# Decode attention on one Trainium2 core: TensorE's code made smaller and brought in by an early jump, with the first load held until TensorE has begun

## The chip, the cores and the metric

The kernel runs on one core of one Trainium2 chip. The metric is the device time of one execution in microseconds; a lower time is better. A kernel was run several times, always beside runs of the kernel before on the same chip. A profile is one execution, so its numbers belong to one run and not to the median run. The span of a profile is about 1.4 us shorter than the measured time of the same execution (before: span 1291.5 us, median time 1292.9 us).

Names: TensorE (PE) multiplies, and PEld is its weight load; VectorE is DVE, ScalarE is ACT, GpSimd is POOL and SyncE is SP. The profile's page counts 16 DMA engines. A *transfer* here is one load issued by SyncE, and a *packet* is one entry of the trace's DMA list, taken as one piece of a transfer on one DMA engine. For keys and values a packet is 64 KiB, and each transfer has 128 of them and ends with 16 completion packets of 4 bytes, taken here as one for each engine. The trace does not name the engine of a packet. So "the latest engine" below is the last of the 16 completion packets of a transfer, and that each engine takes a fixed share of every transfer (128 / 16 = 8 packets) is a reading: it fits these counts and a lateness that stays the same over hundreds of microseconds (in the kernel before the latest engine is 1.57 us late at 238.0 us and 1.56 at 1263.6).

## The reference

```python
def reference(A_x, A_k_cache, A_v_cache, A_wq, A_wo, B_x, B_w1, B_b1, B_w2, B_b2):
    def _A_ref(x, k_cache, v_cache, wq, wo):           # x: 8 x 1 x 576, caches: 8 x 32 x 4096 x 128
        q = (x @ wq).reshape(B, Sq, H, Dh).transpose(0, 2, 1, 3)
        scores = jnp.einsum("bhqd,bhkd->bhqk", q, k_cache) * (Dh ** -0.5)
        p = _softmax(scores, axis=-1)
        o = jnp.einsum("bhqk,bhkd->bhqd", p, v_cache)
        return o.transpose(0, 2, 1, 3).reshape(B, Sq, H * Dh) @ wo
    def _B_ref(x, w1, b1, w2, b2):                     # w1: 576 x 4608, w2: 4608 x 576
        y = _layernorm(x, axis=-1)
        return _gelu(y @ w1 + b1) @ w2 + b2
    x = A_x
    xn = _layernorm(x, axis=-1)
    return x + _A_ref(xn, A_k_cache, A_v_cache, A_wq, A_wo) + _B_ref(xn, B_w1, B_b1, B_w2, B_b2)
```

All tensors are bf16. The caches are 537 MB of the 557 MB that are read, so this is a kernel of reading memory once.

## The kernel before

SyncE issues every large load, in this order, on one queue: the query weights, the weights of the first layer, then keys and values of tiles 0 to 31, then the second layer's weights and the output weights in four parts. All of them land in one buffer (`ring`) that holds about three of the large transfers (keys or values of one tile), so a load is issued only when an older one has been used up.

```python
    od.load("sync", "wq", ring[:, 0:WQ_END], wq_v)       # transfer 0, moved ahead of the start barrier
    first = od.name
    od.load("sync", "w1", ring[:, W1_AT:RING], w1_v)     # transfer 1
    ahead(nc, ENG.SP, [first, od.name], "InstDrain")
    load_kv(k_v, 0, 0)                                   # transfer 2: keys 0
    # ...
    for token in (wq_read, *head_done):                  # the query weights have been read
        od.wait("sync", token)
    load_kv(v_v, 0, 1)                                   # transfer 3: values 0
    for token in mlp_done:                               # the whole head is done
        od.wait("sync", token)
    for t in range(1, NT):
        sy.wait_ge(sem["kf"], NX * (t - 1) + 2)          # TensorE has eaten 2 of 8 blocks of keys t-1
        load_kv(k_v, t, 0)                               # transfer 4 is keys 1
        sy.wait_ge(sem["vf"], t)                         # TensorE is through with values t-1
        load_kv(v_v, t, 1)                               # transfer 5 is values 1
```

The *head* is the work before the first tile: layer norms, the queries, their broadcast to 128 partitions, and the first layer of the MLP. TensorE's code for it is written out:

```python
    def queries(e):                                      # 36 matmuls; in the trace 4 narrow ones in 0.43 us
        for c in range(WC):
            wv = wq_sb[:, c, :].rearrange("p (x m d) -> p m x d", m=M, d=Dh)
            for m in range(M):
                i = e.matmul(S_ps[0][m * MP:(m + 1) * MP, :], lhsT=xT[:, c, :], rhs=wv[:, m], ...)
    # ...
    for b in range(B):                                   # broadcasts: 8 x 4 matmuls, before the first layer
        # ...
        pe(["q", "sel"], [key], broadcast)
        act([key], [f"qb{b}"], lambda e: e.activation(out=dst, in_=t, func=ACT.Copy))
    head_done = [od.last(e) for e in ("tensor", "vector", "scalar")]
    for c in range(WC):                                  # first layer: 9 x 6 matmuls
        pe(["yT", "w1"], ["h_ps"], lambda e, c=c: layer(e, yT[:, c, :], w1_sb[:, c, :], ...))
```

Then VectorE multiplies each key tile by the queries in 8 blocks (the *products*), TensorE sums them, ScalarE takes the exponentials and TensorE multiplies by the values. TensorE goes over the 32 tiles in a loop. Its last 72 + 8 + 64 matmuls are the second layer and the output projection.

The softmax here doesn't subtract the row's maximum and nothing guards it: scores larger than these inputs give would overflow.

## Time and profile before

| | before |
|---|---|
| time, median of 6 runs | 1292.91 us (1292.82 to 1293.04) |
| span of the profile | 1291.5 us |
| read from memory | 556.94 MB, 431 GB/s over the span |
| busy: TensorE, VectorE, ScalarE | 57%, 64%, 4% |

The first lines are of the profile's page: its span, the busy share of the DMA engines in 40 slices, and the DMA queues with packets, MB and share of the time of 16 engines.

```profile
span 1291.5 us, 14658 instructions
...
DMA  9999999999999999999999999999999999999998
...
q1 hardware_dynamic: 10368, 556.93, 99.7%
q8 instruction: 3, 0.05, 0.0%
...
q14 instruction: 1, 0.01, 0.0%
```

The load queue (q1) keeps the 16 engines busy for 99.7% of the span. A 64 KiB packet takes 2.418 us in the trace, so 16 engines move 16 x 65,536 B / 2.418 us = 434 GB/s, and nothing but the two ends and the unevenness of the engines is left to win. The lines "instruction" are the packets whose kind in the trace is "instruction", taken here as code that is brought to an engine. The trace has their times in the span: three of 16 KiB at 29.93, 75.96 and 1287.07 us, each taking 1.0 to 1.1 us, and one of 8 KiB at 52.15 us, taking 0.31 us.

The next view cuts the end into stretches of 0.5 us. The columns are the length, then the busy time of PE, PEld, DVE, ACT and POOL with the number of instructions, TensorE's granted clock, the mean busy share of the DMA engines, and GB/s.

```profile
1287.20:1287.70 0.50, 0.18 (x4) 0.00 (x0) 0.00 (x0) 0.00 (x0) 0.00 (x0) 1.00 0.18 74
1287.70:1288.20 0.50, 0.00 (x0) 0.00 (x0) 0.00 (x0) 0.00 (x0) 0.00 (x0) 1.00 0.19 74
1288.20:1288.70 0.50, 0.39 (x8) 0.30 (x10) 0.00 (x0) 0.00 (x0) 0.00 (x0) 1.00 0.07 28
```

A share of 0.18 or 0.19 is 3 engines of 16. So for the last microsecond of loading 13 engines are done and three are not. The packets show since when. The table holds how late each engine completes a transfer, against the median of the 16; only the four latest are shown.

```
kernel before, completion of a transfer by its latest four engines, us over the median of 16
transfer 1 (first-layer weights)   25.1 us:  0.15  0.20  0.21  0.46
transfer 2 (keys 0)                44.5 us:  0.15  0.16  0.41  1.41
transfer 3 (values 0)              63.8 us:  0.12  0.13  1.31  1.41
transfer 4 (keys 1)                83.2 us:  0.10  1.31  1.42  1.53
transfer 12                       238.0 us:  0.14  1.35  1.45  1.57
```

After each of the first three instruction packets (29.9, 52.2, 76.0 us) one more engine is 1.3 to 1.5 us late. It stays late to the end (0.13, 1.34, 1.45, 1.56 us at 1263.6 us). This fits the fixed share read above and a queue that never pauses (busy for 99.7% of the span), so that it cannot catch up.

The chain of work that ended last shows what this costs (start, duration, what):

```profile
1259.74 28.52 DMA ring<-in_A_wo_dram
1288.26 0.04 issue
1288.31 1.29 PE acc L374 x18
```

TensorE waits until 1288.26 us for a part of the output weights, and 18 matmuls, a cast and the store follow. What the latest engine loses there is lost for the kernel: in the profile after the change this landing is 1.43 us later and the span 1.4 us longer.

Last, the times at which SyncE issues its loads, and the head's main steps. These lines are of the timeline (start, duration, engine, line, operation).

```profile
0.00 0.38 SPq L96 DMA_DIRECT2D ring<-in_A_wq_dram  x1
...
53.53 0.33 SPq L271 DMA_DIRECT2D ring<-in_A_k_cache_dram  x1
74.24 0.33 SPq L271 DMA_DIRECT2D ring<-in_A_v_cache_dram  x1
```

```profile
13.84 4.01 PE L367 MATMUL s_ps<-ring 128*32 128x512 bf16 x36 [1.36 <-DVE quad L354]
...
18.55 0.41 PE L394 MATMUL oT_ps<-ring 128*64 128x256 bf16 x4 [0.36 <-ACT ring L385]
...
26.02 0.85 PE L414 MATMUL o_ps<-ring 128*32 128x384 bf16 x3 [2.80 <-DMA ring<-in_B_w_dram]
...
46.82 6.70 DVE L559 TENSOR_TENSOR ring<-ring,qb 128x4096 bf16<-128x4096 bf16 x3 [0.32 <-DVE hT_sb L445]
```

The queries take 4 us, the broadcasts start at 18.55 us while the first layer's weights are still on their way (they land at about 25.6 us), and VectorE's first product starts at 46.82 us. Keys 1 are issued at 53.53 us. The first engine is through with the transfer before it (values 0) at 63.48 us, so the queue has a *margin* of 63.48 - 53.53 = 9.95 us. Values 1 have 82.81 - 74.24 = 8.57 us. In the steady state the margins are 10.2 and 8.8 us.

### The profile page before, as it was taken

The numbers are of one execution on the slowest core, as the hardware profiler recorded it, in microseconds if no ns is written. First come the engines' busy times: TensorE is split into PE (matmuls) and PEld (weight loads), VectorE is DVE, ScalarE is ACT, GpSimd is POOL, SyncE is SP. The second block draws the span as 40 slices with busy tenths as digits, with TensorE's granted clock in tenths as the row PEclk, the third lists the DMA queues.
The fourth block names the chain that finished last, engine by engine and source line by source line (L and its number), as shares of the span: only waits on it lengthen the run. The fifth ranks groups of instructions, "written<-read, shape, count | busy, mean of one in ns | idle before, by whom it ended". The sixth has DMA issues, their size and how long they took to land. (4 is left out here: it accounts for less than half of the span.)

```text
span 1291.5 us, 14658 instructions
## 1 busy us (share of the span) xinstructions
PE 736.8 (57%) x4707; PEld 322.3 (25%) x4707; DVE 829.4 (64%) x740; ACT 56.8 (4%) x181; POOL 2.4 (0%) x12
## 2 busy tenths in 40 slices
PE   4654565554565554665554565554566554565557
PEld 1222232222222222222222232222222222222223
DVE  2655677655677655677655677655677655577654
ACT  2000000000000000000000000000000000000000
POOL 0000000000000000000000000000000000000000
PEclk8778887778887777887777887778887777888779
DMA  9999999999999999999999999999999999999998
GB/s 419 441 427 440 430 428 449 422 428 449 422 428 449 422 430 447 422 436 440 424 436 438 426 438 434 428 442 428 428 449 422 428 449 422 428 449 422 430 447 350
DMA packets 10410, 557.02 MB, mean 431 GB/s; under 512 B 1163, under 2 KB 1188, under 8 KB 1446
## 3 DMA queue, kind: packets, MB, share of 16 engines
q1 hardware_dynamic: 10368, 556.93, 99.7%
q8 instruction: 3, 0.05, 0.0%
q10 hardware_dynamic: 38, 0.02, 0.0%
q14 instruction: 1, 0.01, 0.0%
HBM read 556.94 MB, written 0.01 MB: 431 GB/s over the span
## 5 line engine op out<-in xcount | busy, mean ns | idle before, releaser
L643 PE MATMUL s_ps<-ring,ident 128*128 x2048 | 544.5, 423 | 514.1 <-PEq L641 513.1
L559 DVE TENSOR_TENSOR ring<-ring,qb 128x4096 bf16<-128x4096 bf16 x256 | 579.2, 2283 | 281.6 <-DMA ring<-in_A_k_cache_dram 281.3
L643 PEld LDWEIGHTS s_ps<-ring,ident 128*128 128x128 bf16 x2048 | 217.4, 106 | 828.3 <-issue 678.5
L534 DVE TENSOR_REDUCE sc<-s_ps 128x32 f32<-128x512 f32 x256 | 171.8, 684 | 0.0
L662 PE MATMUL o_ps<-ring,ebd 128*32 128x512 bf16 x2048 | 116.4, 380 | 0.0
L546 DVE TENSOR_TENSOR ebd<-es,head 128x1536 bf16<-128x1536 bf16 x64 | 77.9, 1218 | 0.0
L569 DVE RECIPROCAL rec<-tot_ps 128x8 f32<-128x8 f32 x32 | 6.6, 208 | 110.7 <-PE oT_ps L670 110.7
L582 ACT ACTIVATE es<-sc 128x192 bf16<-128x192 f32 x64 | 19.8, 310 | 1104.2 <-DVE sc L534 1104.2
L662 PEld LDWEIGHTS o_ps<-ring,ebd 128*32 128x32 bf16 x2048 | 51.6, 97 | 62.5 <-issue 13.6
L670 PE MATMUL oT_ps<-selc,ob 128*128 128x8 f32 x256 | 33.9, 259 | 12.3 <-ACT ob L586 12.3
L670 PEld LDWEIGHTS oT_ps<-selc,ob 128*128 128x128 f32 x256 | 31.0, 191 | 15.2 <-ACT ob L586 15.2
L586 ACT ACTIVATE ob<-o_ps 128x512 f32<-128x512 f32 x32 | 19.1, 597 | 80.2 <-PE o_ps L662 80.2
L425 DVE TENSOR_SCALAR ring<-ring 96x384 f32<-96x384 f32 x2 | 0.7, 352 | 26.4 <-ACT ring L424 26.4
L545 DVE TENSOR_TENSOR Es<-Ep 128x1 f32<-128x1 f32 x32 | 5.1, 160 | 13.3 <-ACT es L582 13.3
L666 PEld LDWEIGHTS tot_ps<-headf,Es 128*128 128x128 f32 x64 | 9.5, 187 | 13.6 <-issue 13.6
L666 PE MATMUL tot_ps<-headf,Es 128*128 128x8 f32 x64 | 12.4, 266 | 0.0
L582 ACT ACTIVATION_READ_ACCUMULATOR es<-sc 128x1 f32 x64 | 11.9, 186 | 0.0
L414 PE MATMUL o_ps<-ring 128*32 128x384 bf16 x27 | 7.8, 860 | 2.8 <-DMA ring<-in_B_w_dram 2.8
L574 DVE TENSOR_TENSOR Ox<-on,quad 128x32 bf16 x32 | 6.2, 192 | 4.8
L414 PE MATMUL s_ps<-ring 128*32 128x384 bf16 x27 | 7.9, 862 | 0.0
L374 PE MATMUL acc<-ring,hT_sb 128*8 128x288 bf16 x72 | 6.0, 335 | 2.8 <-DMA ring<-in_B_w_dram 2.8
L336 PE MATMUL tot_ps<-ident,ring 40*128 40x16 bf16 x9 | 0.7, 204 | 11.8 <-DVE ring L314 11.8
(76 smaller groups left out, 61.2 us busy)
## 6 DMA issues: line engine op xcount, KB each, us to landing
ring<-in_B_w_dram SPq DMA_DIRECT2D x2, 5184.0 KB, 25.2
ring<-in_A_wq_dram SPq DMA_DIRECT2D x1, 4608.0 KB, 13.7
ring<-in_A_wo_dram SPq DMA_DIRECT2D x1, 1728.0 KB, 28.6
ring<-in_A_wo_dram SPq DMA_DIRECT2D x1, 1584.0 KB, 26.5
ring<-in_A_wo_dram SPq DMA_DIRECT2D x1, 1008.0 KB, 28.5
ring<-in_A_k_cache_dram SPq DMA_DIRECT2D x32, 31.9
ring<-in_A_v_cache_dram SPq DMA_DIRECT2D x32, 30.5
ring<-in_A_wo_dram SPq DMA_DIRECT2D x1, 288.0 KB, 28.8
```

Source lines behind the costliest of these rows:

```text
L414: i = e.matmul(h_ps[j][s * MP:(s + 1) * MP], lhsT=lhsT, rhs=wv[:, r0:r0 + HK, :], **flags)
L534: ins = ve.tensor_reduce(out=sc[:, n * CB:(n + 1) * CB], in_=bank_of(x).rearrange("p (c d) -> p c d", d=DL), axis=AX.X, op=ALU.add)
L546: ve.tensor_tensor(out=ebd[:, ja:jb], in0=es[:, a:b].rearrange("p (j c) -> p j c", c=4).unsqueeze(2) .to_broadcast([P, nj, G, 4]), in1=hea ...
L559: ve.tensor_tensor(out=k, in0=k, in1=qb[:, bass.ds(t, 1), :].to_broadcast([P, CB, Dh]), op=ALU.mult,).then_inc(sem["prod"], 1)
L569: ve.reciprocal(out=rec[:], in_=tot_ps[:, :G]).then_inc(sem["rec"], 1)
L574: ve.tensor_tensor(out=Ox[:, bass.ds(t, 1)].rearrange("p o g m -> p (o g) m"), in0=on[:].unsqueeze(2).to_broadcast([P, G, M]), in1=quad[:] ...
L582: sa.activation(out=es[:, a * CB:b * CB], in_=sc[:, a * CB:b * CB], func=ACT.Exp, scale=scale, accum_out=Ep[:, i:i + 1]).then_inc(sem["x"], 1)
L586: sa.activation(out=ob[:].rearrange("r c d -> r (c d)"), in_=o_ps, func=ACT.Copy).then_inc(sem["ob"], 1)
L643: ins = te.matmul(to, lhsT=idn, rhs=k[:, :, d * DL:(d + 1) * DL], start=(d == 0), stop=(d == Dh // DL - 1))
L662: ins = te.matmul(o_ps[m * MP:(m + 1) * MP, :], lhsT=ebd[:, j].rearrange("p g c -> p (g c)"), rhs=vals[:, c:c + 4, :], start=(j < M), stop ...
L666: te.matmul(tot_ps[:, :G], lhsT=Es[:].to_broadcast([P, P]), rhs=headf[:], start=True, stop=True).then_inc(sem["vf"], 1)
L670: ins = te.matmul(oT_ps[:, :G], lhsT=ob[:, c, :], rhs=selc[:, c, :], start=(c == 0), stop=(c == 3))
```

## The change

The intent is to bring TensorE's code in before the first load takes the DMA engines, so that no instruction packet falls among the loads (four do in the kernel before, at 29.93, 52.15, 75.96 and 1287.07 us). The change makes TensorE's code smaller with two register loops, jumps at the start to the last block and back, gives hints where the code of TensorE and VectorE ends, and lets SyncE's first load wait for TensorE's first instruction. The broadcasts move behind the first layer. The diff is cut to its core:

```diff
-    HS, HJ = 3, 2                                     # ... first layer in 6 groups of 384 columns
+    HK = NB // P                                      # ... now 5 groups, of 512 and one of 256 columns
+    te.sem_inc(sem["go"])                             # TensorE's first instruction
+    tensor_last = nc.mark_branch_hint_location(ENG.PE)
+    vector_last = nc.mark_branch_hint_location(ENG.DVE)
+    go = nc.sync.wait_ge(sem["go"], 1).ins.name
     od.load("sync", "wq", ring[:, 0:WQ_END], wq_v)
-    ahead(nc, ENG.SP, [first, od.name], "InstDrain")
+    ahead(nc, ENG.SP, [go, first, od.name], "InstDrain")
@@ queries: a loop; full-width matmuls on zero-padded weights
-        for c in range(WC):
-            for m in range(M):
-                i = e.matmul(S_ps[0][m * MP:(m + 1) * MP, :], lhsT=xT[:, c, :], rhs=wv[:, m], ...)
+                e.matmul(S_ps[0], lhsT=xTz[:, bass.ds(at + (M - 1 - m) * MP, P)], rhs=wv[:, m], ...)
+        (at, w), close = looped("queries", WC - 1, at=(M * MP, M * MP), w=(HQ, HQ))
+        part(at, w, False)
+        close()
@@ broadcasts: a loop of 8 turns, after the first layer
+    def broadcasts(e):
+        (at,), close = looped("broadcast", B, at=(0, MQ))
+        e.wait_ge(sem["free"], 1).then_inc(sem["free"], -1)
+        for v in range(2):
+            for k in reversed(range(NG)):
+                i = e.matmul(t[:(k + 1) * MQ, v * NH2:(v + 1) * NH2, :],
+                    lhsT=selz[:, bass.ds(at + (v * B + 1 - k) * MQ, (k + 1) * MQ)], rhs=q_v[:, k], ...)
+        i.then_inc(sem["full"], 1)
+        close()
@@ the end of the code
-    te.br("head")
+    te.br("tour")                                     # jump to the last block first
+    ve.br("vector_end").branch_hint(vector_last)
+    te.br("tensor_end").branch_hint(tensor_last)
+    block("tour")
+    later(main.bb, nc.cur_bb.bb, ENG.PE)              # TensorE's part of the start barrier stands here
+    te.br("head")
+    block("tensor_end")
```

## The prediction

> **What bounds the kernel now.** The DMA. The page gives 431 GB/s over the 1291.5 us span, 9 in all but one DMA slice, and the load queue 99.7% of 16 engines' time. A 64 KiB packet takes 2.42 us, so 16 engines move 433 GB/s and the 556.9 MB need 1286 us. TensorE is busy 57%, VectorE 64%, which waits 281 us for keys (waits view). Only the ends and the lateness of single DMA engines are left to win.
>
> **What the change aims at.** The DMA-queue part of the page lists instruction packets: three of 16 KiB on queue 8, at 29.9, 76.0 and 1287.1 us by the trace's packets, and one of 8 KiB on queue 14 at 52.2. [...] After each of the first three, one more DMA engine is late: landings lie within 0.5 us at 25 us, then one is 1.4 us behind at 44, two at 64, three (1.35, 1.45, 1.57 us) at 83, and so to the end[...]. In the windows view 3 of 16 engines (share 0.18) still work from 1287.2 to 1288.2. The last chain is: output weights land at 1288.26, 1.29 us of matmuls, a 0.45 us cast, the store. The fetches cost about 1.4 us of it.
>
> The change shrinks TensorE's code (about 790 instructions to 679[...]), jumps to its last block first, hints the ends of TensorE's and VectorE's code, and holds the first load until TensorE starts, so that fetches use idle DMA engines.
>
> **Costs.**
> - Hold: the first load issues at 0.00, TensorE's first instruction stands at 0.32. Estimate +0.35 us, not hidden.
> - The barrier waits for TensorE's jump[...]; keys 0 is queued at 1.26 and needed at 25: hidden.
> - Head: query matmuls lose their four-way concurrency (four in 0.43 us), 4 us become about 13, ending near 27; the first layer starts at 27 to 29 instead of 26 and takes 13 us as before. The broadcasts (5.3 us, before hidden behind the w1 load) come after it, in a register loop of some 1.3 us a turn, tied to ScalarE's 0.6 us copies. VectorE's first product moves from 46.8 to about 54 us. Slack: keys 1 are issued at 53.5 with the queue busy to 63.8, values 1 at 74.2 with it busy to 83.2; less 1 us from issue to packet, 7 to 8 us is hidden, just what I expect. Estimate +0.3 us of bubble on average, up to 3.
>
> **Sum.** 1292.9 - 1.4 + 0.35 + 0.3 = 1292.15; I lean a little lower, as the hold may cost less: predicted 1291.9 us, 80% range 1290.7 to 1293.6. Faster by over 2%: 0.01; within 2%: 0.98; slower by over 2%: 0.01.
>
> **What shows it right.** No instruction packets between the first load and the end; all 16 engines of the last transfers landing within about 0.5 us; no 3-engine tail in the windows view; the first product near 54 us; values 1 issued before 82.
>
> **What would make it wrong.** VectorE's or another fetch stays: the slowest engine is still 1.4 us late and nothing is won (about 1293.3). The early fetch collides with the first packets. The head slips over 8 us: DMA idles near 64 or 83 us, and the time rises by the excess.

The -1.4 rests on the lateness of the engines in the trace of the kernel before (1.35 to 1.57 us). The estimates start from that trace: +0.35 from TensorE's first instruction at 0.32 us; 13 us for the queries from 36 matmuls in 4.01 us, four in 0.43 us; 1.3 us a turn from ScalarE's copies of 0.60 us; 1 us from issue to packet from the first load (issued at 0.00, first packet at 1.008 us). How 13, 1.3 and +0.3 follow is not said.

## The result, and the profile after

| | before | after |
|---|---|---|
| time, median of 6 runs | 1292.91 us | 1294.17 us |
| lowest to highest | 1292.82 to 1293.04 | 1293.28 to 1297.37 |
| span of the profile | 1291.5 us | 1292.9 us |
| 16 KiB and 8 KiB instruction packets in the span | 3 and 1 | 1 and 0 |

The ratio of the times is 1.0012, with a 95% interval of 0.9999 to 1.0025. Ratios here are the mean time of one kernel's fast runs over that of the other's of the same rounds, so they are not quite the ratio of the medians. The median lies 1.3 us higher and above the predicted range, and the runs scatter over 4 us instead of 0.2. The intervals of all ratios here are 0.0013 to 0.0016 wide to each side (1.7 to 2 us), wider than most differences of this document. That the change is slower rests on the single runs (the fastest after, 1293.28 us, is above the slowest before, 1293.04) and on the traces.

These are the page's lines on the span and the queues after the change:

```profile
span 1292.9 us, 14775 instructions
...
q1 hardware_dynamic: 10368, 556.93, 99.7%
q8 instruction: 1, 0.02, 0.0%
```

One packet is left of four. VectorE's of 8 KiB is gone (it is VectorE's by x_cut against x_cut_hint: there at 49.6 us, not there with VectorE's hint) and so are two of the 16 KiB, TensorE's (none is left in x_small, with TensorE's code cut further). The one left is the early fetch; in the trace it runs from 1.537 to 2.963 us. This is after the first load's packets have started (the first at 1.297 us, nine by 1.537), so the two overlap. The order of events at the start, from the trace's instructions and packets:

```
kernel after, the start
0.203  TensorE adds to "go"
0.283  SyncE issues the first load (0.00 in the kernel before)
0.471  TensorE's jump to its last block; it takes 3.626 us
1.297  the first packets of the first load start
1.537  instruction packet, 16 KiB, takes 1.426 us
4.32   the start barrier releases all engines (1.18 in the kernel before)
```

```
kernel after, completion of a transfer by its latest four engines, us over the median of 16
transfer 0 (query weights)   13.2 us:  0.11  0.20  0.24  0.99
transfer 3 (values 0)        64.1 us:  0.11  0.19  0.23  1.04
```

There is now one late engine and not three, but the latest is still 1.04 us behind, and all 16 have been held back by 0.28 us. At 64 us the latest engine of the kernel after stands at 65.16 us and that of before at 65.26 us. Two of the fetches that are saved lie before this point. They are worth 0.1 us, with the hold and the early fetch taken off.

The second part of the answer is in the issue times of SyncE (timeline), and in the head:

```profile
0.28 0.38 SPq L96 DMA_DIRECT2D ring<-in_A_wq_dram  x1
...
61.35 0.33 SPq L294 DMA_DIRECT2D ring<-in_A_k_cache_dram  x1
82.57 0.33 SPq L294 DMA_DIRECT2D ring<-in_A_v_cache_dram  x1
```

```profile
14.78 10.34 PE L413 MATMUL s_ps<-ring 128*128 128x512 bf16 x36 [2.28 <-DMA ring<-in_A_wq_dram]
...
27.05 1.08 PE L446 MATMUL o_ps<-ring 128*32 128x512 bf16 x4 [1.59 <-DMA ring<-in_B_w_dram]
...
40.90 5.51 PE L468 MATMUL b_ps<-ring 128*128 128x256 bf16 x16
...
47.36 5.50 PE L468 MATMUL b_ps<-ring 128*128 128x256 bf16 x16 [0.95 <-PEq L465]
...
55.10 2.29 DVE L627 TENSOR_TENSOR ring<-ring,qb 128x4096 bf16<-128x4096 bf16 x1 [0.31 <-DVE hT_sb L513]
```

The queries take 10.3 us instead of 4.0. The first layer starts 1 us later and ends about as long after. The broadcasts, which were hidden behind the load of the first layer's weights, now take two stretches of 5.5 us at 40.9 and 47.4 us, with nothing to hide behind. The first product starts at 55.10 us, 8.3 us later than before. Keys 1 are issued 7.8 us later and values 1 8.3 us later. Their margins shrink from 9.95 to 63.68 - 61.35 = 2.33 us and from 8.57 to 83.43 - 82.57 = 0.86 us. VectorE shows the same from the other side: what it waits for between its first product and 112 us, first before, then after (engine, line, what it waits for, us in all, times, longest).

```profile
DVE ring L559 <- DMA ring<-in_A_k_cache_dram: 8.9, 1, 8.9
```

```profile
DVE ring L627 <- DMA ring<-in_A_k_cache_dram: 0.4, 1, 0.4
```

With a margin of 0.86 us the queue runs dry. The first packets of values 1, in the trace, start only 1.21 us after the issue, and they are longer than usual:

```
kernel after, packets of values 1 (64 KiB each): start, duration in us
83.778  3.006
83.849  3.278
83.957  3.233
84.149  2.556
...
84.740  2.713
85.149  2.975          the last of the 16 first packets; all 16 take 2.740 on average
86.702  2.418          the second packets are as usual
```

The engines thus lose time twice: they stand still (0.37 us on average and at most 0.7, if they restart in the order in which they finished), and the 16 first packets take 0.3 us longer on average and up to 0.86 us. The second loss does not need the first. At keys 1, with a margin of 2.33 us, the three engines that finish values 0 first go on without a pause, and still their packets take 2.80, 2.88 and 2.96 us; the longest of that transfer takes 3.46 us, and the mean completion is 0.46 us later there already. The mean completion of values 1 moves by 0.70 us in this one transfer. The latest engine goes from 0.05 us ahead of before (keys 1) to 0.98 us behind. Between 200 and 262 us, in a stretch with no lack of work (margins 9.3 to 10.9 us), another 0.45 us is lost on the latest engine: 91 packets there take over 2.45 us, up to 2.66, while the kernel before has none in that stretch. After that nothing more is lost: the difference of the latest engine is +1.42 us from 470 us to the end.

The windows of the end and the chain of work that ended last answer to the lines shown of before:

```profile
1288.20:1288.70 0.50, 0.50 (x12) 0.24 (x6) 0.00 (x0) 0.00 (x0) 0.00 (x0) 1.00 0.82 325
1288.70:1289.20 0.50, 0.13 (x4) 0.00 (x0) 0.00 (x0) 0.00 (x0) 0.00 (x0) 1.00 0.34 131
1289.20:1289.70 0.50, 0.00 (x0) 0.00 (x0) 0.00 (x0) 0.00 (x0) 0.00 (x0) 1.00 0.11 42
```

```profile
1261.24 28.46 DMA ring<-in_A_wo_dram
1289.69 0.04 issue
1289.74 1.29 PE acc L425 x18
```

The tail of single late engines is still there (0.34, then 0.11), and the same part of the output weights lands at 1289.69 us instead of 1288.26: +1.43 us. The 18 matmuls are the same. So the whole loss of the profiled run (1.4 us of span) was made before 280 us and then carried to the end.

### The profile page after: what moved, and what is told of

The parts are those of the page before. It is cut to its first block, busy times and chain, and to the rows that moved or that the text cites. A ratio compares the mean times of both kernels' runs of the same rounds, so it can differ in the third digit from the quotient of the medians.

```text
span 1292.9 us, 14775 instructions
## 1 busy us (share of the span) xinstructions
PE 741.7 (57%) x4698; PEld 324.8 (25%) x4698; DVE 829.6 (64%) x740; ACT 56.6 (4%) x181; POOL 3.4 (0%) x13
## 3 DMA queue, kind: packets, MB, share of 16 engines
q1 hardware_dynamic: 10368, 556.93, 99.7%
## 5 line engine op out<-in xcount | busy, mean ns | idle before, releaser
L713 PE MATMUL s_ps<-ring,ident 128*128 x2048 | 535.8, 417 | 515.9 <-PEq L711 515.8
L713 PEld LDWEIGHTS s_ps<-ring,ident 128*128 128x128 bf16 x2048 | 214.8, 105 | 824.0 <-issue 670.8
L637 DVE RECIPROCAL rec<-b_ps 128x8 f32<-128x8 f32 x32 | 6.7, 208 | 110.7 <-PE b_ps L740 110.7
L740 PE MATMUL b_ps<-selc,ob 128*128 128x8 f32 x256 | 33.9, 259 | 12.3 <-ACT ob L654 12.3
L740 PEld LDWEIGHTS b_ps<-selc,ob 128*128 128x128 f32 x256 | 31.0, 191 | 15.2 <-ACT ob L654 15.2
L446 PE MATMUL o_ps<-ring 128*32 128x512 bf16 (+1 forms) x40 | 12.8, 1078 | 1.6 <-DMA ring<-in_B_w_dram 1.6
L736 PEld LDWEIGHTS b_ps<-headf,Es 128*128 128x128 f32 x64 | 9.5, 187 | 13.6 <-issue 13.6
L736 PE MATMUL b_ps<-headf,Es 128*128 128x8 f32 x64 | 12.4, 266 | 0.0
L413 PE MATMUL s_ps<-ring 128*128 (+1 forms) x36 | 10.3, 459 | 2.3 <-DMA ring<-in_A_wq_dram 2.3
L468 PE MATMUL b_ps<-ring 128*128 128x256 bf16 (+1 forms) x32 | 11.0, 409 | 0.9 <-PEq L465 0.9
```

What stands on the lines that cost most here:

```text
L413: e.matmul(S_ps[0], lhsT=xTz[:, bass.ds(at + (M - 1 - m) * MP, P)], rhs=wv[:, m], start=start and m == 0, stop=False)
L446: i = e.matmul(h_ps[j][s * MP:(s + 1) * MP], lhsT=lhsT, rhs=wv[:, r0:r1, :], **flags)
L468: i = e.matmul(t[:(k + 1) * MQ, v * NH2:(v + 1) * NH2, :], lhsT=selz[:, bass.ds(at + (v * B + 1 - k) * MQ, (k + 1) * MQ)], rhs=q_v[:, k], ...
L713: ins = te.matmul(to, lhsT=idn, rhs=k[:, :, d * DL:(d + 1) * DL], start=(d == 0), stop=(d == Dh // DL - 1))
L736: te.matmul(tot_ps[:, :G], lhsT=Es[:].to_broadcast([P, P]), rhs=headf[:], start=True, stop=True).then_inc(sem["vf"], 1)
L740: ins = te.matmul(oT_ps[:, :G], lhsT=ob[:, c, :], rhs=selc[:, c, :], start=(c == 0), stop=(c == 3))
```

## The experiments

The theory after this comparison has two parts. First, the late head lets the queue run dry at keys 1 and values 1, and this costs about 1 us or more. Second, the early fetch collides with the first load's packets, so the gain that was hoped for (one late engine fewer at the end) does not come. Rivals were: the hold of the first load costs more than its 0.28 us; instruction packets do not matter for the end at all, so there was never a gain; or the number of late engines matters and not the latest one. Twelve kernels were run. Three batches of four, each on another chip, shared their runs of the kernel before: medians 1292.98, 1292.94 and 1293.05 us, 9 runs each, within 0.6 us.

In the tables "margin" is what was defined above (keys 1 / values 1), and "latest" is the completion of the latest of the 16 engines, minus the same for before.

### Broadcasts written out again: a_unrolled

This is the kernel after, with the broadcast loop replaced by static code as before (but still behind the first layer).

```diff
-        (at,), close = looped("broadcast", B, at=(0, MQ))
-        ...
+        for b in range(B):
+            t = (oT_ps, tot_ps)[b % 2].rearrange("p (g d) -> p g d", d=Dh)
+            e.wait_ge(sem["free"], 1).then_inc(sem["free"], -1)
+            for v in range(2):
+                for k in range(NG):
+                    i = e.matmul(t[k * MQ:(k + 1) * MQ, v * NH2:(v + 1) * NH2, :],
+                        lhsT=sel[:, v * B + b].rearrange("p m q -> p (m q)"), rhs=q_v[:, k], ...)
+            i.then_inc(sem["full"], 1)
```

> The changed kernel with the eight query broadcasts written out again (narrow matmuls, static addresses) instead of the register loop[...]. Theory 1 (the late head starves the DMA): first product near 51 instead of 55.1 us, keys 1 and values 1 issued with over 4 us to spare, no lost time there, 1292.7 to 1293.2 us and no scatter over 0.5 us. Theory 2 (the loss is the hold and the early fetch alone): still 1294 or above.[...]

Measured: 1293.89 us (1293.27 to 1294.09, 5 runs), ratio 1.0006 [0.9992, 1.0019]. The margins rise to 5.62 and 4.25 us, and the step at values 1 is gone: the latest engine is +0.86 us at values 0, +0.74 at values 1 and +0.73 at the end. But the lateness is now there from the start. In this run the early fetch took 2.29 us (1.519 to 3.810 us) and its engine is 1.85 us over the mean from the first landing on. There are also two more fetches of 16 KiB, at 54.5 and 1279.2 us. So the head's lateness explains the step at values 1, but the time does not come back (the expectation of 1292.7 to 1293.2 us was missed), because the collision at the start is larger in this build. The two parts are separate costs.

### No hold: a_nohold

```diff
-    te.sem_inc(sem["go"])
-    go = nc.sync.wait_ge(sem["go"], 1).ins.name
-    ahead(nc, ENG.SP, [go, first, od.name], "InstDrain")
+    ahead(nc, ENG.SP, [first, od.name], "InstDrain")
```

> The changed kernel without the hold of the first load. If the hold costs what it delays: 0.28 us less at the first landings; the fetch of TensorE's block then falls among the load packets and its DMA engine stays 1.2 to 1.4 us late instead of 1.0. Whole time within 0.5 us of the changed kernel, bubbles near 62 and 82 us as before. If the hold protected the first loads well, it is slower by 0.5 us or more.

Measured: 1293.82 us (1293.42 to 1294.54, 4 runs), ratio 1.0006 [0.9990, 1.0021]. The first load is issued at 0.00 us. TensorE's jump now takes 6.57 us, because the instruction packet starts only at 4.762 us, behind packets of the load; its engine is 1.4 us over the mean. The margin of values 1 falls to 0.42 us, the mean completion moves by 1.06 us there and by 0.74 us more between 120 and 180 us (129 packets of over 2.45 us). The latest engine ends at +1.49 us. Without the hold the early fetch is no better placed, so the hold is not what spoils the change. The second loss in a stretch with full margins came again, at another time.

### The kernel before with a later head: b_delay9, b_delay13, b_delay17

Here nothing of the change is taken over. ScalarE makes useless copies at the end of the head, so that the products start later. This is the late head alone.

```diff
+    for _ in range(9):            # 13 in b_delay13, 17 in b_delay17
+        act(["pad"], ["pad"], lambda e: e.activation(
+            out=ob[:].rearrange("r c d -> r (c d)"),
+            in_=qb[:, 0:4, :].rearrange("r c d -> r (c d)"), func=ACT.Copy))
```

> The kernel before with nine idle ScalarE copies at the end of the head, which should move the first product from 46.8 to about 51 us. Theory 1: hidden, since values 1 had 8.6 us to spare: within 0.2 us of the kernel before. Theory 2 says the same.

> The same with thirteen copies, first product near 54 to 55.5 us, as late as in the changed kernel, with nothing else of the change. Theory 1: values 1 are issued with about 1 us or less to spare, the DMA runs dry there and the time rises by 0.5 to 2 us, with scatter. Theory 2: no change, below 1293.2 us.

> The kernel before with seventeen idle ScalarE copies: first product near 56.8 us, values 1 issued about 1.2 us after the first engine has finished keys 1. Theory 1: the DMA runs dry there, 1 to 3 us lost at values 1, 1294 to 1296 us. Theory 2 (nothing to do with the head): 1293.0.

| run | first product, us | margins, us | mean at values 1 | latest, values 0 / values 1 / end | time, us | ratio [95%] |
|---|---|---|---|---|---|---|
| before | 46.82 | 9.95 / 8.57 | | | 1292.9 | |
| b_delay9 | 50.81 | 5.87 / 4.63 | +0.03 | -0.08 / -0.03 / -0.04 | 1292.94 | 1.0000 [0.9984, 1.0015] |
| b_delay13 | 53.81 | 3.02 / 1.81 | +0.32 | -0.03 / +0.09 / +0.08 | 1293.02 | 1.0001 [0.9986, 1.0017] |
| b_delay17 | 56.17 | 1.00 / -0.38 | +2.07 | -0.12 / +1.08 / +0.95 | 1295.42 | 1.0022 [1.0007, 1.0038] |

A head that is 4 us late is free, and one that is 7 us late is still free at the end. This missed the expectation for b_delay13: a rise was expected, and none came, although the mean of the 16 engines went up by 0.44 us. In this profile no engine stood still for more than 0.06 us (taking them again in the order in which they finished). What was lost lies in long packets: 3 of the 16 first packets of keys 1 and 5 of those of values 1 took over 2.45 us (up to 3.2), and so did 50 packets between 104 and 200 us. The other engines fell back towards the three late ones, and the latest lost only 0.08 us. With 9.35 us of delay the queue is empty before values 1 are issued. This is the issue of values 1 in that profile:

```profile
83.58 0.33 SPq L271 DMA_DIRECT2D ring<-in_A_v_cache_dram  x1
```

The first engine had nothing left at 83.21 us. The time rises by 2.5 us, and the four runs scatter from 1293.87 to 1296.89 us (the profiled one is the fastest), as widely as those of the kernel after. The scatter, too, can thus be made by a late head alone. No run of this series has the margins of the kernel after (2.33 / 0.86): they lie between those of b_delay13 and b_delay17.

### Two rows per turn of the loop: a_pairs (failed as a test)

```diff
-        (at,), close = looped("broadcast", B, at=(0, MQ))
-        ...
+        (at,), close = looped("broadcast", B // 2, at=(0, 2 * MQ))
+        for u, ps in enumerate((oT_ps, tot_ps)):
+            t = ps.rearrange("p (g d) -> p g d", d=Dh)
+            e.wait_ge(sem["free"], 1).then_inc(sem["free"], -1)
+            ...
```

> The changed kernel with the broadcast loop turned over four times for two batch rows instead of eight times for one: the two targets become static[...]. Theory 1 (late head starves the DMA at values 1): first product near 51 to 52 us, values 1 issued with 4 us to spare, no step at 82 us and no long packets after it; what is left is the engine made late at the start by the early fetch, 1.0 to 1.8 us, so 1292.6 to 1293.3 us. If the loss is the start alone, it stays at 1294.

Measured: 1293.82 us (1293.63 to 1294.34, 5 runs), ratio 1.0007 [0.9994, 1.0021]. The loop was to be faster and was not: the first product starts at 55.34 us, and the margins are 1.74 and 0.74 us. So the run does not separate the theories. It agrees with the first in that the step is there again (mean +0.84 us at values 1). It has two fetches more than the kernel after (7.8 and 1290.7 us). Why four turns of two rows cost as much as eight of one was not followed up.

### The head made early enough: a_early

This keeps all of TensorE's code, the jump, the hints and the hold. Only VectorE is freed: ScalarE does the last two copies of the head in its place, and VectorE starts tile 0 when the queries of the first batch row are there.

```diff
-        dve([f"s{j}"], [f"hT{j}"], lambda e: e.tensor_copy(out=hT_sb[...], in_=t...))
+        for c in range(k):
+            act([f"s{j}"], [f"hT{j}"], lambda e: e.activation(
+                out=hT[:, c], in_=ps[:, c], func=ACT.Copy))
@@
     for e in ("vector", "scalar", "tensor", "gpsimd"):
-        od.wait("vector", od.last(e))
+        if e in ("vector", "gpsimd"):
+            od.wait("vector", od.last(e))
         od.wait("tensor", od.last(e))
+    nc.vector.wait_ge(sem["full"], 3)
```

> The changed kernel, TensorE's code untouched, but VectorE begins tile 0 as soon as the first batch row's queries are ready: the small hidden-layer copies go to ScalarE and VectorE no longer waits for TensorE's last broadcast. Theory 1: first product near 49 us, values 1 issued 4 us or more before the first engine is free, no step at 82 us, no long packets after it, scatter under 0.5 us. What is left is the hold and one engine made late at the start, which is about as late as the latest engine of the kernel before: 1292.7 to 1293.2 us. If the head is not the cause: 1294 and scatter as in the changed kernel.

Measured: 1292.98 us (1292.85 to 1293.41, 5 runs), ratio 1.0000 [0.9986, 1.0014]. The first product starts at 48.53 us; the margins are 4.02 and 2.78 us. The latest engine is +0.27 us at values 0, +0.15 at values 1 and +0.13 at the end, so the latest engine takes no step, and there is no later loss. The mean of the 16 moves by 0.23 us at values 1: 10 of the 16 first packets take over 2.45 us, up to 3.01, with a margin of 2.78 us and no pause over 0.16 us. The scatter of 4 us is gone. The early fetch (at 1.456 us, taking 1.711 us) is still there, and its engine is 1.36 us over the median at the first landing (0.99 in the kernel after). The last chain of this profile:

```profile
1259.96 28.45 DMA ring<-in_A_wo_dram
1288.40 0.04 issue
1288.45 1.29 PE acc L425 x18
```

It is 0.14 us behind the kernel before (1288.26). This is the main result. a_early differs from the kernel after only in how early the head lets VectorE begin. With that, all that the change loses is gone, and what is left of it is worth nothing. The 1.3 us by which the kernel after is slower are the late head. (The two kernels ran on different chips and are compared through the kernel before. The intervals of their ratios overlap; the single runs, 1292.85 to 1293.41 against 1293.28 to 1297.37 us, hardly do.)

### Is there anything to win? x_cut, x_cut_hint, x_small (results wrong)

In these the kernel before lost work on TensorE, so that its code is short. x_cut keeps one of nine steps of the queries and of the first layer and few of the last matmuls (about 411 instructions by count). x_cut_hint adds the change's hint for VectorE. x_small also drops most broadcasts, the rest of the first layer and most matmuls with the values (about 217 by the same count). The loads are the same in all.

```diff
-        for c in range(WC):                     # queries, first layer
+        for c in range(1):
-        for v, r in parts[:R]:                  # second layer
+        for v, r in parts[:1]:
-        for r in range(r0, r1):                 # output projection
+        for r in range(r0, r1 if n > 1 else r0 + 1):      # n > 2 in x_small
# x_cut_hint and x_small:
+    vector_last = nc.mark_branch_hint_location(ENG.DVE)
+    ve.br("vector_end").branch_hint(vector_last)
+    block("vector_end", ENG.DVE)
# x_small:
+        if b < 2:                               # broadcasts
+            if M <= j < 2 * J - M:              # matmuls with the values
+                continue
```

> Wrong result on purpose: the kernel before, all its loads kept, but eight of nine steps of the query and first-layer products, 34 of 36 of the second layer and 21 of 23 rows of the first two parts of the output product left out, so that TensorE has about 400 instructions, and with the hint for the end of VectorE's code of the changed kernel. If the late engines come from the code fetches: no instruction packet in the span, all 16 engines land within 0.5 us to the end, and the kernel takes 1291.4 to 1291.8 us, 1.2 to 1.5 less than before. If their lateness has another cause: three engines late as before, 1292.9 us.

> The same without the hint on VectorE's code. One 8 KiB instruction packet near 52 us is left, one engine of 16 about 1.3 us late from there to the end, and as the last transfer needs all 16, the whole gain is lost: 1292.7 to 1293.0 us. If lateness adds up over engines, two thirds of the gain should stay: 1291.9.

> Wrong result on purpose: all loads kept, TensorE's work cut to about 210 instructions[...], VectorE's code hinted. If code fetches alone make engines late: no instruction packet between the first load and the end, all 16 engines within about 0.5 us of their median to the end, the last weights packet near 1287.1 us from the start instead of 1288.5. If lateness comes from elsewhere: engines over 1 us late as before.

| run | instruction packets in the span, us | late engines, us over the median | last packet of the loads against before | time, us | ratio [95%] |
|---|---|---|---|---|---|
| x_cut | 49.6 (8 KiB), 73.2 (16 KiB) | two: 1.16, 1.18 | -0.38 | 1293.72 | 1.0006 [0.9990, 1.0021] |
| x_cut_hint | 73.2 (16 KiB) | one: 1.17 | -0.35 | 1293.64 | 1.0006 [0.9992, 1.0019] |
| x_small | none | none (all within -0.42 and +0.32) | -1.23 | 1291.77 | 0.9993 [0.9978, 1.0008] |

The first two missed their expectations: a packet of 16 KiB that was not expected is there in both, and both are slower than forecast. x_small met its own. Three things follow. The hint for VectorE works: the packet of 8 KiB is there without it (49.6 us in x_cut) and gone with it (x_cut_hint). One late engine or two make the same end (-0.35 and -0.38 us), so the latest one counts and not their number. And where no instruction packet is in the span, the loads end 1.23 us earlier and the median time falls by 1.28 us. The page and the windows of x_small show it: no "instruction" line, and no engine at work after 1287.70 us.

```profile
span 1290.4 us, 10613 instructions
...
q1 hardware_dynamic: 10368, 556.93, 99.8%
q10 hardware_dynamic: 38, 0.02, 0.0%
```

```profile
1287.20:1287.70 0.50, 0.30 (x2) 0.00 (x0) 0.00 (x0) 0.00 (x0) 0.00 (x0) 0.50 0.01 5
1287.70:1288.20 0.50, 0.42 (x4) 0.09 (x4) 0.00 (x0) 0.00 (x0) 0.00 (x0) 0.50 0.00 0
```

So the premise of the change holds, and some 1.2 us (0.1%) is all that there is to win. The packets show this better than the time does, because the end of x_small is not that of the kernel before: it waits for the last part of the output weights and then has 4 matmuls at a clock of 0.50, where the kernel before waits for the part before the last and has 18 at 1.00. For that part before the last x_small goes on at 1287.09 us and the kernel before at 1288.31, which is again 1.22 us. One of the four runs of x_small took 1293.08 us and the others 1291.64 to 1291.78; this one run is not explained.

The times of x_cut and x_cut_hint are higher than before although their loads end earlier. For x_cut_hint the windows show that this lies after the loads: TensorE's clock stood at 0.50 from 1287.2 to 1290.4 us (1.00 in the kernel before, from 1287.2 to 1288.7 and over its last 18 matmuls), and its last 18 matmuls took 2.35 us instead of 1.29. From 1280 to 1287.9 us the cut had left it 0.8 us of work instead of 7.2; whether that kept the clock low was not tested.

### The hold alone, and a hold long enough: b_hold, a_fullhold

b_hold is the kernel before with nothing but the wait for TensorE's first instruction. a_fullhold is a_early with "go" given only after the jump has arrived, so that the early fetch is over before the first load is issued.

```diff
# b_hold, against before
+    ahead(nc, ENG.PE, [nc.tensor.sem_inc(sem["go"]).ins.name], "InstDrain")
+    go = nc.sync.wait_ge(sem["go"], 1).ins.name
-    ahead(nc, ENG.SP, [first, od.name], "InstDrain")
+    ahead(nc, ENG.SP, [go, first, od.name], "InstDrain")
# a_fullhold, against a_early
-    te.sem_inc(sem["go"])
     block("tour")
     later(main.bb, nc.cur_bb.bb, ENG.PE)
+    ahead(nc, ENG.PE, [te.sem_inc(sem["go"]).ins.name], "InstDrain")
```

> The kernel before with the hold alone: TensorE's first instruction counts up a semaphore and the first load waits for it. Expected cost 0.25 to 0.3 us at the first landing and at the end, 1293.2 us. If the hold costs nothing (hidden behind other start-up): 1292.9.

> The early-start version of the changed kernel with the first load held until TensorE has fetched its last block and stands in it. The fetch then meets no load: first load at about 3 us or somewhat more, no engine over 0.5 us late at the first landing, none later, so the stretch from the first load to the last weights packet is 1.0 to 1.4 us shorter than in the kernel before. The hold itself costs 2.5 to 4 us, so the whole is 1294 to 1296 us. If the early fetch had not been what makes the engine late, the stretch is no shorter.

b_hold: 1293.39 us (1293.19 to 1293.50, 5 runs), ratio 1.0003 [0.9989, 1.0016]. The first load is issued at 0.273 us, and the mean completions are 0.29 to 0.32 us later from the first to the last. The hold costs what it delays, and no more.

a_fullhold: 1295.90 us (1295.78 to 1296.17, 4 runs), ratio 1.0023 [1.0007, 1.0038]. The instruction packet has the engines to itself, from 1.269 to 2.241 us, and the first load follows at 3.665 us. Now all engines are within -0.31 and +0.39 us of the median from the first landing to the last. From the first issue to the last packet this kernel needs 1287.31 us and the kernel before 1288.53: it wins 1.22 us, as x_small does. But it has paid 3.67 us for it. (The span is 2.5 us longer than before. The measured time is 2.85 us longer; the rest lies outside the span and was not followed up.) The jump alone took 3.22 us, of which the packet is 0.97.

So the early fetch can be kept apart from the loads, and then the whole gain is there; the price of waiting for it is three times the gain. A hold of over about 1.2 us eats it.

### The margins in one table

| run | margins keys 1 / values 1, us | mean completion, step at values 1, us | latest engine, values 0 to values 1, us |
|---|---|---|---|
| b_delay9 | 5.87 / 4.63 | +0.01 | +0.05 |
| a_unrolled | 5.62 / 4.25 | 0.00 | -0.12 |
| a_fullhold | 4.42 / 3.39 | +0.01 | -0.16 |
| a_early | 4.02 / 2.78 | +0.23 | -0.12 |
| b_delay13 | 3.02 / 1.81 | +0.17 | +0.12 |
| after | 2.33 / 0.86 | +0.70 | +1.08 |
| a_pairs | 1.74 / 0.74 | +0.84 | +0.34 |
| a_nohold | 1.95 / 0.42 | +1.06 | +0.71 |
| b_delay17 | 1.00 / -0.38 | +1.77 | +1.20 |

The kernel before moves its own latest engine by 0.12 us here, with its third fetch, so -0.12 means no step. With a margin for values 1 of 3.39 us or more nothing is seen. From 2.78 us down the mean suffers; below 1 us the latest engine does, and with it the kernel. The mean suffers before the queue runs dry. Of the 16 first packets of keys 1, none is over 2.45 us long at margins of 4.02 to 5.62 us (a_early, a_fullhold, a_unrolled), and one of 2.55 us is at 5.87 (b_delay9); 3 are at 3.02 us (b_delay13), 14 at 2.33 (after) and 14 at 1.00 (b_delay17, where no engine pauses for more than 0.11 us). Why a load that is issued so late has long first packets stays open. What a given run loses below 1 us is not a smooth function of the margin.

One more reading keeps these runs honest. In the profiles of a_unrolled, a_pairs and b_delay13 the last chain does not wait for the output weights: TensorE's first 36 matmuls of the end took 4.48 us instead of 3.67, and it worked without a pause from the landing of the second layer's weights. From that landing to the last matmul it took 11.67 to 11.68 us there and 11.70 us in the kernel before. The landing moves with the latest engine in the same way (a_unrolled: 1278.65 against 1277.90 us), so the comparison stands, but the two ends of this kernel are nearly equally long.

## Why the prediction was wrong

The number was 1291.9 us with a range up to 1293.6, and 1294.17 was measured. Point by point:

- *What bounds the kernel*: right. It is the DMA, and only the latest engine of the end could be won. x_small shows the size: 1.23 us at the last packet, where the prediction said "about 1.4".
- *Costs, hold +0.35*: right. The first load was issued at 0.28 us, and b_hold lost 0.34 us.
- *Head, first product near 54 us*: right in mechanism and nearly in size, 55.10 us. The queries took 10.3 us and not 13; the broadcasts took 12.6 us, 1.57 us a turn on average, and not 1.3 us a turn (1.36 us in the last turns; in between ScalarE had the first layer's functions to do, from 44.34 to 46.57 us).
- *VectorE's fetch goes*: right, shown by x_cut (a packet of 8 KiB at 49.6 us) against x_cut_hint (none).
- *The sum's term -1.4*: this step failed. The prediction counted the fetches as gone. The early one is still there, and a hold of 0.28 us does not keep it apart from the first load: the load's packets start 1.01 us after its issue, the instruction packet starts at 1.54 us. Its engine is 1.0 us over the mean (1.3 to 1.85 us in a_early, a_nohold and a_unrolled). Together with the hold the latest engine was 0.1 us ahead of before at 64 us. This was named among the risks ("The early fetch collides with the first packets"), but the sum gave it no weight. a_early, which has this collision and no bubble that reaches the latest engine, equals the kernel before, where hold and saved fetches were to make it 1.05 us faster. a_fullhold shows that without the collision the term is right (1.22 us).
- *The sum's term +0.3 for bubbles*: this step failed too, and it made the rise. The slack was taken as "7 to 8 us", from margins of 9.95 and 8.57 us less 1 us from issue to packet, and the head's slip came out at 8.3 us, just beyond it. The slack was mis-sized, because it counted standstill alone. The first packet came 1.2 us after the issue of values 1, and with a margin under about 3 us the first packets are already stretched, from 2.42 to 2.74 us on average here, so that by estimate only some 5.5 to 7 us of the slip were free (the two margins of before less 3). It cost the latest engine 1.08 us at values 1 and another 0.45 us between 200 and 262 us. The risk as written ("the time rises by the excess") would have made 0.3 us of a slip of 8.3. The prediction's text had "up to 3" for this term; as an average it was too low, and the range was drawn around the average.

The sum with measured terms, on the latest engine of the profiled run: -0.10 (fetches saved, collision and hold together, at 64 us), +1.08 (values 1), +0.45 (200 to 262 us), which makes 1.43 us. The chain's landing moved by 1.43 us and the span by 1.4.

What stays open: why packets are long again after 120 or 200 us with full margins (after, a_nohold, and less of it in b_delay13 and a_pairs; neither before nor a_early has it, and b_delay17, whose queue ran dry for longest, has none either, so a dry queue alone does not explain it); which part of the code each fetch brings, and why a_pairs fetches at 7.8 us; and the loop of a_pairs. The 1.3 us of the medians are explained by the runs with the late head, but the trace explains one run of 1294.42 us, not the one of 1297.37.

No version beats the kernel before. a_early equals it, and a_unrolled, a_pairs and a_nohold lie 0.8 to 0.9 us above it.

## What to carry to other kernels

When work before a stream of loads is moved, list for each load the time between its issue and the moment when the queue runs dry, and keep more of it than the time from issue to first packet (1.21 us at values 1 of the kernel after): here 4 us was free (a_early at keys 1, 4.02 us), packets grew long at 3 us (b_delay13, 3.02 us), under 1 us the kernel paid (after, 0.86 us), and the loss did not come back in this kernel, whose load queue is busy for 99.7% of the span (latest engine +1.42 us from 470 us to the end). Here a transfer ended with its latest DMA engine, so taking away two of three latenesses of about the same size won little (0.35 us at the last packet in x_cut_hint, against 1.23 us for all in x_small); the last one paid. A wait that clears the way for something else must cost less than what it clears: here a hold of 3.7 us bought 1.2 us.
